# Chunked attention and a SoLU feed-forward layer on one core: the first two tiles take unsplit float32 weights

## The chip, the core and the metric

The kernel runs on one core of a Trainium2 chip. Its engines are TensorE (PE; its weight loads are listed as PEld), VectorE (DVE), ScalarE (ACT), GpSimd (POOL) and SyncE (SP, which here only issues transfers); 16 DMA engines move data. The metric is the device time of one execution in microseconds (us).

## The reference

For each of 8 x 8 heads, 576 rows are cut into nine chunks of 64; each chunk attends to itself only. The 4608 x 512 result goes through a feed-forward layer with SoLU and a layer norm.

```python
scores = scale * np.matmul(q_c, k_c.transpose(0, 1, 2, 4, 3))    # 64 x 64 per chunk
attn = softmax(scores);  out = np.matmul(attn, v_c)              # q, k, v: (8, 8, 576, 64) float32
x = np.ascontiguousarray(attn_out.transpose(0, 2, 1, 3)).reshape(B * S, H * D)   # 4608 x 512
h = x @ w_in                                                     # 512 x 1024
sm = e / (np.sum(e, axis=-1, keepdims=True) + 1e-09);  solu = h * sm
ln = (solu - mu) / np.sqrt(var + 1e-06) * g_ln
return (ln @ w_out).astype(np.float32)                           # 1024 x 512
```

w_in and w_out arrive as 64-bit floats and are turned into float32 on the chip; q, k, v and g_ln are 32-bit.

## The kernel before

**Tiles.** 36 tiles of 128 rows (two chunks each). For one tile: q and k are turned on TensorE (`nat` to `qT`, `kT`), the scores go to `sx` or `sy` in PSUM, VectorE and ScalarE make the softmax in `e`, TensorE turns it (`attn_t`), and a product with `v_sb` gives the tile of x, turned, again in `sx` or `sy`. The first product with w_in fills `ph` (two PSUM banks, one buffer); SoLU reads `ph` three times (VectorE's maximum `h_nmax`, ScalarE's exponential, VectorE's product into `z`), and only then may the next tile write `ph`. z is turned (`z_t` by transfers, or on TensorE for tiles 0, 1 and 35), and the second product, with w_out scaled by g, goes to `po`, in thirds of eight instructions. The store scales by `r` into `o_sb`.

**Split products.** TensorE's one-pass mode (fp32r) drops low bits, so each operand is held as two fp32r halves: x as `x_h`, `x_l`, w_in as `wi_h`, `wi_l`, w_out as `wo_h`, `wo_l`, z as `z_h`, `z_l`. A product is three passes: high by low, high by high, low by high. One tile takes 24 instructions of 128 x 512 for `ph` and 24 for `po`.

**Weights.** They come in eight parts called units: 0 to 3 are 128 rows of w_in, 4 to 7 are 256 rows of w_out, 1 MB each in `w_raw`. A unit is clipped (`unit_scale`, first half, on GpSimd), passed through Prelu (ScalarE), shifted and rounded to float32 in `w_a` (`unit_round`, VectorE), copied to its high part (`unit_high`, ScalarE), and the two low halves are the differences (`unit_rest`, VectorE).

**Order.** Each engine works strictly in the order in which the program issues. For tiles 0 to 4 and the weights this order is the string `START`: each word is a step, and a word that stands again continues the step where it yielded. `n` loads q and k of a tile, `v` its v, `P` a unit; `N` turns q or k, `S` scores, `A`, `B` the softmax (B's last part divides by the sum, "the norm"), `T` turns e, `V` the product with v and x's halves, `c`, `C`, `t`, `D` the four steps of a unit, `M` the first product, `X`, `Y` SoLU, `R` the variance, `z` and `Z` turn z, `F` a third of the second product, `o` the store, `U` prepares later tiles, `Q`, `q` load q and k of a later batch into `q_st`, `k_st`, `g` loads g_ln. "M:2" is M of tile 2, "D:3:1" the second low half of unit 3. From tile 5 on a loop issues all work: the first product of tile i, then three thirds for an earlier tile.

The tables `NV_DVE`, `MEAN_POOL`, `TV_DVE` and others say for single steps of the start whether VectorE, ScalarE or GpSimd takes them. `nat` has two buffers, so n:i waits until N:(i-2) is done; a unit's `w_raw` takes a place in the buffers of later tiles (`z_b`, `z_t`, `q_st`, `k_st`).

All instructions that the wrapper `Ordered` passes on carry one line in the profile, L49, that of the wrapper.

Of the kernel before, what the change touches and what calls it, by code (L numbers as in the profile page):

```python
# [57 lines left out]
def chunk_attention_then_solu_ffn(  # L58
# [103 lines left out]
    def unit_scale(x):  # L162

        hi = raws[x][:, :, :, 1]
        y = scaled[x] = work.tile([P, 2, HALF], F32, name="w_a", bufs=4)
        top = 1.875 * 2.0 ** 16  # L170
# [4 lines left out]
        act.activation(y, y, AF.Prelu, scale=2.0 ** -112, alpha=-(2.0 ** 32))

    def unit_round(x):
# [4 lines left out]
        kind, m = UNITS[x]  # L182
        if kind == "out" and m == 0:
            dve.tensor_scalar(
                out=g_sb, in0=g_sb, scalar1=1.0 / FF, scalar2=None, op0=ALU.mult
            )
# [505 lines left out]
    def product():  # L692
# [6 lines left out]
        "v": load_v, "g": load_g, "Q": load_batch, "q": load_some,  # L699
# [128 lines left out]
```

## Time and profile before

| what | us |
|---|---|
| median of 3 runs | 489.1 (488.9 to 489.53) |
| the profiled execution | 489.85 |
| its span, first to last instruction | 488.0 |
| TensorE busy | 466.7 (96%) |
| VectorE busy | 376.2 (77%) |
| ScalarE busy | 252.2 (52%) |
| GpSimd busy | 136.6 (28%) |

A row of the timeline has the start in us, the duration in us, the engine, the line, the operation, the tile written and the tiles read, the size, and how many instructions were merged; in brackets stands how long the engine idled before it and what ended that. "SPq" and "ACTq" are issues of transfers. Matmuls overlap, so the pace of TensorE is read from the distance of two starts.

### The profile page before, as it was taken

Reading aid. Unit: us, or ns where it says so; the run is one execution under the profiler, and the core shown is the slowest. Engines: PE = TensorE matmul, PEld = TensorE weight load, DVE = VectorE, ACT = ScalarE, POOL = GpSimd, SP = SyncE. Lnnn points to the kernel's source line nnn. Section 1 sums busy time; section 2 is a strip of 40 time slices with the busy share of each in tenths; the row PEclk is TensorE's granted clock in tenths of the full one; section 3 lists DMA queues with packets and bytes.
Section 4 is the critical chain, followed back from the end, with each engine's and each line's share of the span. In section 5 each row is a group of like instructions: output and inputs, shape, how many; then the busy total and the mean of one; then the engine's idle time right before and its main releaser. Section 6 shows DMA issues by size and latency. Waiting matters only on the chain.

```text
span 488.0 us, 11335 instructions
## 1 busy us (share of the span) xinstructions
PE 466.7 (96%) x4352; PEld 384.8 (79%) x4352; DVE 376.2 (77%) x525; ACT 252.2 (52%) x406; POOL 136.6 (28%) x287
## 2 busy tenths in 40 slices
PE   4599998999999999999999999999999999999996
PEld 3477886688888888888888888888888888888875
DVE  2989996797969797979797979797979797945420
ACT  3647872654546454546454545454545555554451
POOL 1302213332323232323232323232414141413300
PEclk9979999999999999999999999999999999999999
DMA  9999989569696887696538596949653534333211
GB/s 262 296 259 253 147 143 195 129 101 208 131 191 128 177 173 188 120 201 128 147 77 188 116 203 128 197 100 196 142 131 90 129 96 123 100 96 108 65 44 43
DMA packets 195909, 72.59 MB, mean 149 GB/s; under 512 B 180048, under 2 KB 180560, under 8 KB 195472
## 3 DMA queue, kind: packets, MB, share of 16 engines
q1 hardware_dynamic: 189008, 58.49, 55.2%
q0 software_dynamic: 6272, 12.60, 9.9%
q8 instruction: 34, 0.56, 0.5%
q10 hardware_dynamic: 576, 0.79, 0.5%
q14 instruction: 19, 0.16, 0.1%
HBM read 37.23 MB, written 9.44 MB: 96 GB/s over the span
## 4 chain that ended last, share of the span: by engine, by line
PE 82%; SPq 6%; DMA 4%; DVE 4%; ACT 2%; issue 1%; POOL 0%; ACTq 0%
PE po L49 39%; PE ph L49 36%; SPq L49 6%; PE sx L49 4%; DMA nat<-in_k_dram 3%; PE sy L49 3%; DMA k_st<-in_k_dram 1%; DVE h_nmax L49 1%; ACT z L49 1%; DVE e L49 1%; DVE z L49 1%; DVE w_a L49 0%; DVE s_sum L49 0%; ACT o_sb L49 0%; ACT wo_h L49 0%
## 5 line engine op out<-in xcount | busy, mean ns | idle before, releaser
L49 PE MATMUL ph<-wi_l,x_h 128*128 128x512 f32 x288 | 113.8, 395 | 0.3 <-DVE z L49 0.3
L49 PE MATMUL ph<-wi_h,x_h 128*128 128x512 f32 x288 | 113.0, 392 | 0.0
L49 PE MATMUL po<-wo_l,z_h 128*128 128x512 f32 x280 | 111.2, 397 | 0.1
L49 PE MATMUL po<-wo_h,z_l 128*128 128x512 f32 x280 | 109.5, 391 | 0.0
L49 PE MATMUL po<-wo_h,z_h 128*128 128x512 f32 x280 | 109.4, 391 | 0.0
L49 ACT ACTIVATE z<-ph,h_nmax 128x1024 f32<-128x1024 f32 x36 | 40.2, 1116 | 132.2 <-DVE h_nmax L49 132.1
L49 PE MATMUL ph<-wi_h,x_l 128*128 128x512 f32 x288 | 78.7, 392 | 0.0
L49 POOL DMA_DIRECT2D z_t<-z_b x136 | 67.6, 505 | 28.5 <-DVE z_b L49 24.5
L49 POOL TENSOR_TENSOR u<-ssq,eps 128x1 f32<-128x1 f32 x36 | 7.4, 205 | 230.4 <-ACT sq L49 230.3
L49 DVE TENSOR_REDUCE h_nmax<-ph 128x1 f32<-128x1024 f32 x36 | 44.0, 1223 | 34.6 <-PE ph L49 34.6
L49 PEld LDWEIGHTS ph<-wi_l,x_h 128*128 128x128 f32 x288 | 54.6, 190 | 12.0 <-ACT x_h L49 0.5
L49 PEld LDWEIGHTS ph<-wi_h,x_l 128*128 128x128 f32 x288 | 54.6, 190 | 11.5
L49 PEld LDWEIGHTS ph<-wi_h,x_h 128*128 128x128 f32 x288 | 54.7, 190 | 11.2
L49 PEld LDWEIGHTS po<-wo_l,z_h 128*128 128x128 f32 x280 | 52.5, 188 | 11.8 <-ACT z_h L49 0.5
L49 PEld LDWEIGHTS po<-wo_h,z_l 128*128 128x128 f32 x280 | 52.6, 188 | 11.4 <-DVE z_l L49 0.4
L49 PEld LDWEIGHTS po<-wo_h,z_h 128*128 128x128 f32 x280 | 52.6, 188 | 10.4
L49 DVE TENSOR_TENSOR z_l<-z_t,z_h 128x1024 fp32r<-128x1024 f32 (+1 forms) x35 | 40.7, 1163 | 21.6 <-ACT z_h L49 21.6
L49 ACT ACTIVATE z<-z,z_sum 128x1024 f32<-128x1024 f32 x35 | 40.4, 1153 | 29.6 <-DVE z L49 23.9
L49 DVE SCALAR_TENSOR_TENSOR z<-ph,z 128x1024 f32<-128x1024 f32 x36 | 43.9, 1220 | 12.8 <-ACT z L49 12.7
L49 DVE STREAM_TRANSPOSE z_b<-z 128x1024 f32<-128x1024 f32 x33 | 40.0, 1211 | 8.0 <-ACT z L49 7.8
L49 ACT ACTIVATE o_sb<-po,r 128x512 f32<-128x512 f32 (+1 forms) x37 | 24.7, 668 | 30.4 <-POOL r L49 20.2
L49 ACT ACTIVATE sq<-z 128x1024 bf16<-128x1024 f32 x36 | 37.5, 1043 | 0.0
(70 smaller groups left out, 591.0 us busy)
## 6 DMA issues: line engine op xcount, KB each, us to landing
out_dram<-o_sb SPq DMA_DIRECT2D x33, 256.0 KB, 2.5
v_sb<-in_v_dram SPq DMA_DIRECT2D x32, 256.0 KB, 4.4
z_t<-z_b SPq DMA_DIRECT2D x128, 64.0 KB, 2.9
z_t<-z_b POOLq DMA_DIRECT2D x128, 64.0 KB, 2.7
q_st<-in_q_dram SPq DMA_DIRECT2D x96, 72.0 KB, 3.3
k_st<-in_k_dram SPq DMA_DIRECT2D x96, 72.0 KB, 3.2
w_raw<-in_moe_w_out_dram SPq DMA_DIRECT2D x4, 1024.0 KB, 7.3
attn_t<-a_b SPq DMA_DIRECT2D x60, 64.0 KB, 3.9
```

The lines of the kernel that those rows point to most:

```text
L49: ins = make(*args, **kwargs)
```

## The change

- The first product of tiles 0 and 1 (`FM = 2`) reads the rounded float32 weights `w_a` directly, in float32, with an unsplit x (`x_f`): 8 instructions of 128 x 512 in place of 24. Tile 0's are issued in four parts, by 128 rows of w_in. The splitting of w_in comes behind them in the order; it is first used by tile 2. `w_a` has five buffers in place of four, and unit 3 takes the buffer of `z_b`.
- g_ln is loaded as eight rows on ScalarE's queue, turned on TensorE and scaled by 1/1024 from there; before, SP loaded it with one element per descriptor.
- The stores of tiles 0 and 1 go to SP as steps of their own; before, ScalarE issued them.
- GpSimd takes eleven of the low halves (`SUB_POOL`) and the norm of five tiles (`NORM_POOL`); VectorE takes two of the clippings (`CL_DVE`). `MEAN_POOL` and `TV_DVE` are emptied.
- Sixteen products of `ident` with itself into `ph` (`W`) stand among the first turns.
- `START` is a new order.

```diff
-    NV_DVE = ((1, 0), (6, 0), (8, 0), (9, 0), (9, 1),)
-    MEAN_POOL = (1,)
-    CL_DVE = ()
-    TV_DVE = (5,)
-    SUB_POOL = ()
-    NORM_POOL = ()
+    NV_DVE = ((0, 1), (1, 0), (1, 1), (7, 1), (9, 0),)
+    MEAN_POOL = ()
+    CL_DVE = (2, 6,)
+    TV_DVE = ()
+    SUB_POOL = ((0, 0), (1, 1), (2, 0), (2, 1), (3, 0), (3, 1), (4, 0), (4, 1), (5, 0), (7, 0), (7, 1),)
+    NORM_POOL = (1, 3, 4, 5, 7,)
+    XV_DVE = (1,)
+    FM = 2
...
+        tag, bufs = ("z_b", 1) if x == 3 else ("w_a", 5)
+        y = scaled[x] = work.tile([P, 2, HALF], F32, name="w_a", tag=tag, bufs=bufs)
...
     def start_values(i):
         values(i)
         yield
+        if i < FM:
+            x_whole(i)
+            return
...
+    def x_whole(i):
+        x = work.tile([P, NCC, P], F32, name="x_f", tag="x_h")
+        to = x.rearrange("p a (c t) -> p a c t", t=CH)
+        of = attn(i, 1).rearrange("p c a t -> p a c t")
+        if i in XV_DVE:
+            dve.tensor_copy(out=to, in_=of)
+        else:
+            act.copy(to, of)
+        st[i, "x"] = x, None
...
-        sums = [(n, cc, m) for n in range(2) for cc in range(NCC) for m in range(3)]
+        if i < FM:
+            ops = [(xh, None)]
+        else:
+            ops = [(xh, wi_l), (xh, wi_h), (xl, wi_h)]
...
             pe.matmul(
-                ph[:, n, :], x[:, cc, :], w[:, cc, cols],
+                ph[:, n, :], x[:, cc, :], scaled[cc][:, n] if w is None else w[:, cc, cols],
...
+    def warm(x):
+        if not idle:
+            idle.append(ps_h.tile([P, 2, HALF], F32, name="ph"))
+        for n in range(2):
+            pe.matmul(
+                idle[0][:, n, x % 4 * P:(x % 4 + 1) * P], ident, ident, start=True, stop=True
+            )
...
+    def start_store(i):
+        store(i)
+        yield
+        for to, of in stores:
+            sync.dma_start(to, of)
+        stores.clear()
...
-        sync.dma_start(g_sb, g_ln.rearrange("(a p) -> p a", p=P))
+        act.dma_start(g_row, g_ln.rearrange("(a p) -> a p", p=P))
+
+    def turn_g():
+        pt = bank()[:, :NFC]
+        pe.transpose(pt, g_row, ident[:NFC, :NFC])
+        yield
+        dve.tensor_scalar(out=g_sb, in0=pt, scalar1=1.0 / FF, scalar2=None, op0=ALU.mult)
```

What `START` and the tables make of each engine's order is shown at three places. The wrapper's line is L49 before and L50 now.

**TensorE, from the turns of tile 2 to the first products into `ph`** (`e_98`, `e_99`, `e_100` are the two softmax buffers; `ident` is the identity). Before:

```order
L49 MATMUL po<-ident,nat 128x128 x8
L49 MATMUL po<-ident,e_98 64x64 x16
L49 MATMUL sx<-kT,qT 64x64 x16
L49 MATMUL sy<-attn_t,v_sb 64x64 x16
L49 MATMUL po<-ident,nat 128x128 x8
L49 MATMUL ph<-wi_l,x_h 128x512
L49 MATMUL ph<-wi_h,x_h 128x512
```

Now:

```order
L50 MATMUL sy<-attn_t,v_sb 64x64 x16
L50 MATMUL po<-ident,e_100 64x64 x16
L50 MATMUL ph<-ident 128x128 x2
L50 MATMUL sx<-kT,qT 64x64 x16
L50 MATMUL ph<-w_a,x_f 128x512 x4
L50 MATMUL sy<-attn_t,v_sb 64x64 x16
L50 MATMUL po<-ident,nat 128x128 x4
L50 MATMUL po<-ident,e_99 64x64 x16
L50 MATMUL po<-ident,nat 128x128 x4
L50 MATMUL ph<-w_a,x_f 128x512 x4
```

Before, tile 0's first product stands behind the turns of tile 3 and reads split weights. Now its first half stands behind the scores of tile 3, and its second half behind the turns of tile 4, whose two groups stand between the halves.

**GpSimd, the steps of the start.** Before, the eight clippings and then only small steps:

```order
L355 MEMSET e_99 128x8
L49 TENSOR_SCALAR w_a<-w_raw 128x1024 x8
L49 TENSOR_SCALAR z<-z,z_sum 128x1024
L49 TENSOR_TENSOR u<-ssq,eps 128x1
L49 TENSOR_TENSOR r<-u,mhalf 128x1
```

Now, from the clippings of units 4 and 5 to that of unit 7:

```order
L50 TENSOR_SCALAR w_a<-w_raw 128x1024 x2
L50 TENSOR_TENSOR wi_l<-w_a,wi_h 128x512
L50 TENSOR_SCALAR w_a<-w_a,g_sb 128x512
L50 TENSOR_TENSOR wo_l<-w_a,wo_h 128x512
L50 TENSOR_TENSOR e_99<-e_99,s_rinv 128x8x64
L50 TENSOR_TENSOR wi_l<-w_a,wi_h 128x512 x3
L50 TENSOR_TENSOR e_100<-e_100,s_rinv 128x8x64
L50 TENSOR_SCALAR w_a<-w_a,g_sb 128x512
L50 TENSOR_TENSOR wo_l<-w_a,wo_h 128x512
L50 TENSOR_SCALAR w_a<-w_a,g_sb 128x512
L50 TENSOR_TENSOR wo_l<-w_a,wo_h 128x512
L50 TENSOR_SCALAR w_a<-w_raw 128x1024
```

The norms of tiles 4 and 5 (`e_99`, `e_100`) stand among subtractions, and the clipping of unit 7 behind all of these.

**SP, the later loads of the start.** Before:

```order
L49 DMA q_st<-in_q_dram 32x18x32 x8
L49 DMA k_st<-in_k_dram 32x18x32 x8
L49 DMA v_sb<-in_v_dram 128x8x64
L49 DMA nat<-in_q_dram 128x8x64
L49 DMA nat<-in_k_dram 128x8x64
L49 DMA k_st<-in_k_dram 32x18x32 x8
L49 DMA nat<-in_q_dram 128x8x64
L49 DMA nat<-in_k_dram 128x8x64
```

Now:

```order
L50 DMA nat<-in_q_dram 128x8x64
L50 DMA nat<-in_k_dram 128x8x64
L50 DMA q_st<-in_q_dram 32x18x32 x16
L50 DMA v_sb<-in_v_dram 128x8x64
L50 DMA nat<-in_q_dram 128x8x64
L50 DMA nat<-in_k_dram 128x8x64
L50 DMA k_st<-in_k_dram 32x18x32 x16
L50 DMA out_dram<-o_sb 128x512
L50 DMA z_t<-z_b 32x512 x8
```

Before, the q and k of tile 8 stand between the two halves of the k_st loads and those of tile 9 behind them; now tile 9 stands ahead of all q_st loads, tile 8 ahead of all k_st loads, and the store of tile 0 stands between these and the transfers of z.

More of the change, by code (lines that the diff above doesn't have):

```diff
@@ L121, in chunk_attention_then_solu_ffn @@
     g_sb = const.tile([P, NFC], F32, name="g_sb")
+    g_row = const.tile([NFC, P], F32, name="g_row")
     const.tile([P, 336], F32, name="pad")
@@ L168, in unit_scale @@
         hi = raws[x][:, :, :, 1]
-        y = scaled[x] = work.tile([P, 2, HALF], F32, name="w_a", bufs=4)
+        tag, bufs = ("z_b", 1) if x == 3 else ("w_a", 5)
+        y = scaled[x] = work.tile([P, 2, HALF], F32, name="w_a", tag=tag, bufs=bufs)
         top = 1.875 * 2.0 ** 16
@@ L177, in unit_round @@
     def unit_round(x):
[L182 to L186, printed above, removed]
         lo = raws.pop(x)[:, :, :, 0]
-        a = scaled.pop(x)
+        a = scaled[x]
         au = a.bitcast(U32)
-        dve.tensor_scalar(
+        (pool if x in SH_POOL else dve).tensor_scalar(
             out=au, in0=au, scalar1=3, scalar2=None, op0=ALU.logical_shift_left
@@ L197, in unit_round @@
         )
-        tops[x] = a
     def unit_high(x):
         kind, m = UNITS[x]
-        a = tops[x]
+        a = scaled[x]
         if kind == "in":
@@ L210, in unit_high @@
                 act.activation(top[:, y], a[:, y], AF.Copy, scale=g)
-        tops[x] = a, top
+        tops[x] = top
     def unit_rest(x, y):
         kind, m = UNITS[x]
-        a, top = tops[x]
+        a, top = scaled[x], tops[x]
         g = None
@@ L463, in ffn_in @@
         ph = st[i, "h"] = ps_h.tile([P, 2, HALF], F32, name="ph")
-        sums = [(n, cc, m) for n in range(2) for cc in range(NCC) for m in range(3)]
+        if i < FM:
+            ops = [(xh, None)]
+        else:
+            ops = [(xh, wi_l), (xh, wi_h), (xl, wi_h)]
+        last = len(ops) - 1
+        sums = [(n, cc, m) for n in range(2) for cc in range(NCC) for m in range(len(ops))]
         if i == 0:
@@ L471, in ffn_in @@
         for at, (n, cc, m) in enumerate(sums):
-            if i == 0 and at and at % 6 == 0:
+            if i == 0 and at and at % (2 * len(ops)) == 0:
                 yield
             cols = slice(n * HALF, (n + 1) * HALF)
-            x, w = ((xh, wi_l), (xh, wi_h), (xl, wi_h))[m]
+            x, w = ops[m]
             pe.matmul(
-                ph[:, n, :], x[:, cc, :], w[:, cc, cols],
-                start=(cc == 0 and m == 0), stop=(cc == NCC - 1 and m == 2),
+                ph[:, n, :], x[:, cc, :], scaled[cc][:, n] if w is None else w[:, cc, cols],
+                start=(cc == 0 and m == 0), stop=(cc == NCC - 1 and m == last),
+            )
+    idle = []
+    def warm(x):
[4 more added lines that the diff above has]
+                idle[0][:, n, x % 4 * P:(x % 4 + 1) * P], ident, ident, start=True, stop=True
             )
@@ L624, in store @@
             stores.append((out[i * P:(i + 1) * P, cols], o[:, cols]))
-        if not order.on or i >= NT - 3:
+        if order.on and i >= NT - 3:
             store_rest()
+    def start_store(i):
[4 more added lines that the diff above has]
+        stores.clear()
     stores = []
@@ L698, in chunk_attention_then_solu_ffn @@
         "P": load_pair, "P0": load_first, "P1": load_second, "n": load_natural,
[L699 removed]
+        "v": load_v, "g": load_g, "G": turn_g, "Q": load_batch, "q": load_some,
         "N": turn_natural, "S": scores, "A": start_softmax, "B": softmax_b,
@@ L702, in chunk_attention_then_solu_ffn @@
         "C": unit_round, "t": unit_high, "D": unit_rest, "M": ffn_in, "X": solu_a, "Y": solu_b,
-        "R": variance, "Z": z_turn, "z": z_half, "F": product, "o": store,
+        "R": variance, "Z": z_turn, "z": z_half, "F": product, "o": start_store, "W": warm,
     }
```

26 lines of the change are left out of this document (14 added, 12 removed).

## The prediction, made before the change was timed

> **What bounds the kernel now.** I read the page first (busy shares, then the slices), then the windows, and only then single rows.
>
> ```profile
> PE 466.7 (96%) x4352; PEld 384.8 (79%) x4352; DVE 376.2 (77%) x525; ACT 252.2 (52%) x406; POOL 136.6 (28%) x287
> PE   4599998999999999999999999999999999999996
> ```
>
> TensorE is busy 466.7 of 488.0 us, and the slices with a low digit are the first two or three and the last. The windows give what is missing there (columns: stretch, its length, busy time and count of PE, PEld, DVE, ACT, POOL, granted clock, DMA share, GB/s).
>
> ```profile
> 0.00:10.00 10.00, 3.72 (x43) 3.19 (x44) 0.69 (x1) 3.12 (x4) 1.96 (x11) 1.00 0.92 236
> 10.00:20.00 10.00, 6.56 (x81) 5.07 (x79) 9.74 (x13) 6.14 (x9) 2.44 (x2) 1.00 1.08 357
> 20.00:30.00 10.00, 6.63 (x82) 5.29 (x81) 9.92 (x15) 5.76 (x8) 1.54 (x1) 0.73 1.05 219
> 80.00:90.00 10.00, 7.05 (x66) 5.43 (x65) 9.65 (x16) 2.97 (x7) 4.16 (x8) 1.00 0.69 182
> 120.00:474.00 354.00, 353.92 (x3145) 292.78 (x3144) 277.89 (x386) 180.26 (x291) 106.49 (x230) 1.00 0.60 136
> ```
>
> From 120 to 474 us TensorE never rests, and the change leaves the program there as it is. So the change is worth what it does to the moment at which the loop's first product into `ph`, that of tile 5 (M:5), begins; everything behind it moves along. I follow TensorE to that moment.
>
> ```profile
> 26.07 1.09 PE L49 MATMUL po<-ident,nat 128*128 128x128 f32 x4 [0.82 <-DMA nat<-in_k_dram]
> 27.38 0.63 PE L49 MATMUL ph<-wi_h,x_h 128*128 128x512 f32 x1
> 27.81 0.63 PE L49 MATMUL ph<-wi_h,x_l 128*128 128x512 f32 x1
> ...
> 34.53 0.39 PE L49 MATMUL ph<-wi_h,x_h 128*128 128x512 f32 x1
> 34.76 0.40 PE L49 MATMUL ph<-wi_h,x_l 128*128 128x512 f32 x1
> ...
> 41.16 0.47 PE L49 MATMUL ph<-wi_l,x_h 128*128 128x512 f32 x1 [0.26 <-DVE z L49]
> ...
> 46.90 0.63 PE L49 MATMUL po<-ident,nat 128*128 128x128 f32 x4
> ...
> 51.00 0.50 PE L49 MATMUL ph<-wi_l,x_h 128*128 128x512 f32 x1
> ...
> 83.27 0.63 PE L49 MATMUL po<-ident,nat 128*128 128x128 f32 x4 [2.03 <-DMA nat<-in_q_dram]
> ...
> 86.67 0.66 PE L49 MATMUL po<-ident,nat 128*128 128x128 f32 x4 [0.91 <-DVE qT L49]
> ...
> 91.63 0.66 PE L49 MATMUL po<-ident,nat 128*128 128x128 f32 x4 [0.18 <-ACT kT L49]
> 92.04 0.48 PE L49 MATMUL ph<-wi_l,x_h 128*128 128x512 f32 x1
> ```
>
> Starts matter, not durations: 27.38 to 27.81 is 0.43 us for one 512-wide product, 34.53 to 34.76 is 0.23, so the clock was still half when M:0 began near 27. M:1 runs 41.16 to 46.90, M:2 begins at 51.00, M:5 at 92.04. Between M:2 and M:5 TensorE waits 2.03 + 0.91 + 0.18 = 3.1 us.
>
> **The change part by part.** *Loads.* What M:0 waits for is read where GpSimd takes up each unit of w_in (c:0 to c:3).
>
> ```profile
> 8.20 1.10 POOL L49 TENSOR_SCALAR w_a<-w_raw 128x1024 f32<-128x1024 f32 x1 [6.76 <-DMA w_raw<-in_moe_w_in_dram]
> 13.01 1.21 POOL L49 TENSOR_SCALAR w_a<-w_raw 128x1024 f32<-128x1024 f32 x1 [3.71 <-DMA w_raw<-in_moe_w_in_dram]
> 17.78 1.23 POOL L49 TENSOR_SCALAR w_a<-w_raw 128x1024 f32<-128x1024 f32 x1 [3.57 <-DMA w_raw<-in_moe_w_in_dram]
> 20.40 1.54 POOL L49 TENSOR_SCALAR w_a<-w_raw 128x1024 f32<-128x1024 f32 x1 [1.39 <-DMA w_raw<-in_moe_w_in_dram]
> 31.52 4.95 SPq L49 DMA_DIRECT2D g_sb<-in_moe_g_ln_dram  x1
> ```
>
> The last two lie 2.62 us apart with one unit between them; the steps before are 4.8 with a unit and a tile's q and k. So a unit costs 2.6, q and k of a tile 2.15, and v (half of that) 1.1, and the engines carry them one behind the other (DMA share 0.92 to 1.08). Tile 0 and unit 0 were there at 8.2. In the new queue order (n0 n1 w0 w1 n2 v0 n3 w3 w2 v1 n4 v2 n5) this makes: n1 7.7, w1 12.9, n2 15.0, n3 18.3, w3 20.9, w2 23.5, v1 24.6, n4 26.7, n5 30.0. The same rule puts the old n3 at 23.6 where the row says 26.07, because later loads share the engines: I keep up to 2.5 us for that in the range. g by rows moves off SP, where it held the queue for 4.95 us; the loads behind it then go out with no gap.
>
> *M:0.* Now it needs units that are scaled and rounded, not split. The last unit (w2) goes through these:
>
> ```profile
> 9.33 1.06 ACT L49 ACTIVATE w_a<-w_a 128x1024 f32<-128x1024 f32 x1 [1.30 <-POOL w_a L49]
> ...
> 15.60 0.64 DVE L49 TENSOR_SCALAR w_a<-w_a 128x1024 uint32<-128x1024 uint32 x1
> 16.76 1.30 DVE L49 SCALAR_TENSOR_TENSOR w_a<-w_raw,w_a 128x1024 uint16<-128x1024 uint32 x1
> 29.30 2.50 DVE L49 TENSOR_TENSOR wi_l<-w_a,wi_h 128x512 fp32r<-128x512 f32 x4
> ```
>
> Clipping on VectorE like the shift 0.65, Prelu 1.06, shift 0.64, rounding 1.3: 3.7 us, and about 1.6 of a softmax and a norm ahead in VectorE's queue: ready near 28.9, unit 3's rounding 1.3 later. The eight low-part halves at 0.62 (2.50/4) that stood before M:0 go behind it.
>
> One unsplit product is not in the trace. The program's other float32 products show two records for each (32 for 16), 64 columns wide:
>
> ```profile
> 57.31 0.66 PE L49 MATMUL po<-ident,nat 128*128 128x128 f32 x4
> 57.89 1.15 PE L49 MATMUL po<-ident,e 64*64 64x64 f32 x32
> 58.97 0.66 PE L49 MATMUL po<-ident,nat 128*128 128x128 f32 x4
> 59.56 0.69 PE L49 MATMUL sx<-kT,qT 64*64 64x64 f32 x32
> 60.07 0.65 PE L49 MATMUL sy<-attn_t,v_sb 64*64 64x64 f32 x32
> ```
>
> Sixteen turns of e take 58.97 - 57.89 = 1.08, 0.068 each; eight times the width gives 0.54 if they run one by one, 1.08 if its two quadrant pairs run side by side. Four passes of the 0.23 product lie between, at 0.91; I take that, since two records at a half-wide array point to the upper half. A tile is then 8 x 0.91 = 7.3 (4.3 to 8.6) against 24 x 0.23 = 5.5. So M:0's last two quarters run 28.9 to 32.5, where the old M:0 ended at 37.26 (below): 4.8 us earlier. Its first half (3.6 us near 23) has 2 us of slack before the 27 at which n4's turns follow. The 16 warm-up products fill waits for loads; at the slow pace they cost at most 16 x 0.43 = 6.9 us, about the 3.4 + 3.4 us that TensorE is idle in the second and third windows. If the clock is half anyway, M:0's tail takes 3.6 longer.
>
> *M:1 and the hold on `ph`.* `ph` has one buffer, so tile i+1 waits for three steps of tile i:
>
> ```profile
> 37.26 1.23 DVE L49 TENSOR_REDUCE h_nmax<-ph 128x1 f32<-128x1024 f32 x1 [1.65 <-PE ph L49]
> ...
> 38.52 1.12 ACT L49 ACTIVATE z<-ph,h_nmax 128x1024 f32<-128x1024 f32 x1 [0.18 <-DVE h_nmax L49]
> ...
> 39.79 1.22 DVE L49 SCALAR_TENSOR_TENSOR z<-ph,z 128x1024 f32<-128x1024 f32 x1
> ```
>
> From 37.26 to M:1 at 41.16 are 3.9 us. New: 32.5 + 3.9 + 7.3 = 43.7 for the end of M:1 (old 46.90). Then 24 turns (0.58 per four, from 58.97 to 59.56), one sx, one sy (0.51 each) and an e stand ahead of M:2: 24/4 x 0.5 + 1.0 + 1.1 = 5.0. M:2 at 48.7, 2.3 earlier.
>
> *M:2 to M:5.* Old 41.04. The 3.1 us of waits go: two of them come from the store of tile 0 on ScalarE's queue and the loads behind it:
>
> ```profile
> 78.57 0.37 ACTq L632 DMA_DIRECT2D out_dram<-o_sb  x1
> 78.99 1.15 ACT L49 ACTIVATE z<-z,z_sum 128x1024 f32<-128x1024 f32 x1 [5.21 <-DMA k_st<-in_k_dram]
> ```
>
> ScalarE stood 5.2 us behind that store's issue, which now stands on SP, where the next rows (halves of z_t) are wanted only behind M:5; tile 8's load now stands ahead of all k_st loads and tile 9's ahead of q_st. From the rows of the order, this stretch also loses two nat groups (1.2), an e (1.1), an sx and an sy (1.0) and gains a group of z turns (0.5): 2.8. So 35.2, and M:5 at 83.9: 8.1 earlier.
>
> *GpSimd's new work* is what must hide. It gets eleven subtractions, five of them with a scaling ahead, and five norms; VectorE loses 16 x 0.62 = 10 us net of small additions. A two-input step of 128x512 on GpSimd is not in the trace; the nearest row is its one-input step of twice the width:
>
> ```profile
> L49 POOL TENSOR_SCALAR w_a<-w_raw 128x1024 f32<-128x1024 f32 x8 | 9.9, 1234 | 40.4 <-DMA w_raw<-in_moe_w_in_dram 15.4 <-DMA w_raw<-in_moe_w_out_dram 14.2 <-ACT attn_t L49 6.7
> ```
>
> Half of 1.234 is 0.62 (T at least); twice that for two inputs is 1.24; twice again where VectorE gets in the way, 2.5. I take 1.24, the row read element for element over both inputs. The scaling counts T/2. Its longest chain starts when ScalarE has made wo_h of unit 4: ten ScalarE steps behind tile 0's exponential (34.8), half of them as wide as the row at 38.52 (1.1 us), half of half that width, 8.6 in all, and 0.8 of hand-overs: 44.2. From there 9.5 T pass until the first third of F:0 has its low parts, then c:7 (1.2), unit 7's Prelu, shift, rounding and scaled copy (4.2), and 3 T before the last third: with the 12.7 us of products from M:4 to M:5 and 1.2 for what lies between, M:5 can't be before 63.5 + 12.5 T. At 1.24 that is 79.0, hidden by 4.9 us; from T = 1.63 it sets the end, from 2.28 the change loses.
>
> **Sum.** -4.8 (M:0) + 1.6 (M:1's products) + 0.9 (what stands ahead of M:2) - 5.8 = -8.1 us. A new order has waits of its own; I charge 1.5, half of what the old one had. That leaves -6.6: 489.85 - 6.6 = 483.2 for a profiled execution, 482.5 for the median (489.1, 0.75 under the profiled execution).
>
> **Rivals.** *GpSimd becomes the bound* (slower). At T = 2.5 M:5 comes at 94.8, 2.7 late: 491.8; it decides from T = 2.28. For: the chain is long and in order, and norms that TensorE waits for stand behind subtractions. Against: 1.24 needs almost a doubling. 0.09. On this the Trainium skill speaks against the change: "GPSIMD Engine Reference", "Performance versus the Vector engine", has a two-input step take about twice VectorE's time, and "When to use GPSIMD" advises against it; an estimate from VectorE's 0.62 is T = 1.25 and the sum stays, while the port that the page has both engines share would lift it towards this rival, which no row here can show.
>
> *The front is won and partly given back* (gain 1 to 4, 485 to 488). Loads share the engines as the old n3 did (2.5), the clock stays half in M:0 (up to 3.6), or one of the tight places (the norm of tile 4 before M:2, unit 7's low parts) waits: 8.1 - 5 = 3 left, 486. For: DMA shares near 1 up to 80 us. 0.17.
>
> *Nothing moves* because 1.6 + 3.6 us of slow float32 products eat an M:0 that starts no earlier: 489. Against: four units' splitting, 5 us of VectorE, does leave the path. 0.06.
>
> **How the numbers follow.** Forecast 0.68: gain 4 to 10. The low end takes the cheaper float32 product (-3 on M:1) and no new waits, 478.5; the high end the second rival's 3 us less a little, 487.5. Repeats lie within 0.65 us of each other, so 0.2% (1.0 us) is the least that can be told from no change: faster 0.85, same 0.06, slower 0.09.
>
> **What would show it.** M:0's first unsplit product near 23 and its last end near 32.5; 0.91 us from one to the next; M:2 near 49 and M:5 near 84; no 5 us hole in ScalarE at the first store; POOL subtractions of 1.2 us. Wrong would be: M:5 later than 88, or subtractions over 2 us with `wi_l` or `wo_l` named as TensorE's releaser, or a new hole behind 120 us.

## The result: 3.0 us faster, not 6.6

The changed kernel takes 486.35 us (median of 4, 485.87 to 486.58) against 489.31 for the kernel before beside it on the same chip: a ratio of 0.9938, 95% interval 0.9920 to 0.9955, so 3.0 us are gained. The profiled execution takes 486.58 us, its span is 484.8 (before: 489.85 and 488.0).

From the page of the changed kernel, the busy shares and TensorE's slices:

```profile
PE 468.0 (97%) x4369; PEld 382.0 (79%) x4369; DVE 366.6 (76%) x509; ACT 253.1 (52%) x407; POOL 161.6 (33%) x305
PE   5889988999999999999999999999999999999996
```

VectorE lost 9.6 us and GpSimd gained 25. The windows of the changed kernel, with the columns of those shown of before:

```profile
20.00:30.00 10.00, 8.68 (x163) 5.87 (x155) 8.36 (x12) 5.92 (x9) 1.85 (x2) 1.00 1.08 276
...
120.00:474.00 354.00, 353.93 (x3089) 292.76 (x3082) 278.06 (x387) 180.92 (x292) 106.86 (x230) 1.00 0.59 134
```

From 20 to 30 us TensorE is busier and keeps its full clock (0.73 before); behind 120 us nothing changed (TensorE busy 353.92 before, 353.93 now), so the start of M:5 again tells the whole. TensorE of the changed kernel, from M:0 to M:5, with VectorE's first maximum of tile 0 between (timeline; start, duration, what was waited for):

```profile
23.94 3.70 PE L50 MATMUL ph<-w_a,x_f 128*128 128x512 f32 x8
...
29.66 0.63 PE L50 MATMUL po<-ident,nat 128*128 128x128 f32 x4 [0.82 <-DMA nat<-in_q_dram]
31.50 0.63 PE L50 MATMUL po<-ident,nat 128*128 128x128 f32 x4
31.96 3.60 PE L50 MATMUL ph<-w_a,x_f 128*128 128x512 f32 x8
35.40 0.60 PE L50 MATMUL po<-ident,nat 128*128 128x128 f32 x4
...
35.60 1.23 DVE L50 TENSOR_REDUCE h_nmax<-ph 128x1 f32<-128x1024 f32 x1 [2.07 <-PE ph L50]
...
39.39 7.13 PE L50 MATMUL ph<-w_a,x_f 128*128 128x512 f32 x16
46.36 1.04 PE L50 MATMUL po<-ident,nat 128*128 128x128 f32 x8
...
51.64 0.50 PE L50 MATMUL ph<-wi_l,x_h 128*128 128x512 f32 x1
...
62.05 0.50 PE L50 MATMUL po<-wo_l,z_h 128*128 128x512 f32 x1 [1.29 <-POOL wo_l L50]
...
74.95 0.50 PE L50 MATMUL po<-wo_l,z_h 128*128 128x512 f32 x1 [1.67 <-POOL wo_l L50]
...
88.83 0.48 PE L50 MATMUL ph<-wi_l,x_h 128*128 128x512 f32 x1
```

An unsplit product is again two records, so 16 records are eight products: 39.39 to 46.36 is 0.87 us each. M:5 begins at 88.83 instead of 92.04, 3.2 earlier, which is the difference of the spans. Set beside the prediction's steps (us; the end of M:0 is read as it was read for the kernel before, where VectorE begins `h_nmax`):

| step | before | forecast | measured |
|---|---|---|---|
| end of M:0 | 37.26 | 32.5 (-4.8) | 35.60 (-1.7) |
| from there to the end of M:1 | 9.64 | 11.2 (+1.6) | 10.76 (+1.1) |
| from there to M:2 | 4.10 | 5.0 (+0.9) | 5.28 (+1.2) |
| M:2 to M:5 | 41.04 | 35.2, and 1.5 charged (-4.3) | 37.19 (-3.8) |
| sum | | -6.6 | -3.2 |

The first row carries 3.1 of the 3.4 us that are missing. In the last, new waits took 2.96 us where 1.5 was charged, and the rest came out 1.0 better. Two readings of the changed kernel say why.

**The loads.** The first lines are GpSimd's and VectorE's clippings in the timeline, which wait for the units 1, 3 and 2; then the windows in between, whose last two columns are the DMA share and GB/s.

```profile
13.03 1.12 POOL L50 TENSOR_SCALAR w_a<-w_raw 128x1024 f32<-128x1024 f32 x1 [1.43 <-DMA w_raw<-in_moe_w_in_dram]
23.91 1.22 POOL L50 TENSOR_SCALAR w_a<-w_raw 128x1024 f32<-128x1024 f32 x1 [3.27 <-DMA w_raw<-in_moe_w_in_dram]
26.49 0.69 DVE L50 TENSOR_SCALAR w_a<-w_raw 128x1024 f32<-128x1024 f32 x1 [0.33 <-DMA w_raw<-in_moe_w_in_dram]
```

```profile
10.00:12.00 2.00, 1.64 (x11) 1.20 (x9) 1.97 (x4) 0.48 (x1) 1.13 (x1) 1.00 0.95 387
...
14.00:16.00 2.00, 0.91 (x9) 0.74 (x8) 1.97 (x4) 1.58 (x2) 0.15 (x1) 1.00 1.34 222
16.00:18.00 2.00, 2.00 (x41) 1.79 (x39) 1.97 (x4) 1.87 (x3) 0.00 (x0) 1.00 0.82 165
18.00:20.00 2.00, 1.15 (x38) 0.96 (x36) 0.51 (x1) 1.13 (x3) 1.91 (x2) 1.00 0.97 197
20.00:22.00 2.00, 2.00 (x65) 1.81 (x58) 1.74 (x3) 0.48 (x2) 0.63 (x1) 1.00 1.06 377
```

Unit 1 came as forecast (13.0 for 12.9); unit 3 came at 23.9 for 20.9 and unit 2 at 26.5 for 23.5. Where q, k and v run one behind the other (14 to 20 us) the engines move 165 to 222 GB/s, where units run 377 to 387.

**GpSimd.** Its groups of the first 90 us:

```profile
L50 POOL TENSOR_SCALAR w_a<-w_a,g_sb 128x512 f32<-128x512 f32 x5 | 9.2, 1846 | 7.7 <-ACT wo_h L50 7.7
L50 POOL TENSOR_TENSOR wi_l<-w_a,wi_h 128x512 fp32r<-128x512 f32 x6 | 8.1, 1356 | 0.5 <-ACT wi_h L50 0.5
...
L50 POOL TENSOR_TENSOR wo_l<-w_a,wo_h 128x512 fp32r<-128x512 f32 x5 | 6.4, 1276 | 0.4
L50 POOL TENSOR_TENSOR e<-e,s_rinv 128x512 f32<-128x512 f32 x5 | 5.7, 1147 | 11.4 <-DVE s_rinv L50 11.4
```

The subtractions take 1.28 to 1.36 us on the mean, near the assumed 1.24. The scaling by g ahead of a `wo_l`, with one input and a factor per partition, takes 1.85 on the mean (1.56 to 2.19): three times the assumed 0.62, and longer than the step with two inputs. The chain of waits runs through these steps from 45.96 to 74.95.

### The profile page after: what moved, and what is told of

Same layout as the page of the kernel before. It is cut to its first block, busy times and chain, and to the rows that moved or that the text cites. A ratio compares the mean times of both kernels' runs of the same rounds, so it can differ in the third digit from the quotient of the medians.

```text
span 484.8 us, 11379 instructions
## 1 busy us (share of the span) xinstructions
PE 468.0 (97%) x4369; PEld 382.0 (79%) x4369; DVE 366.6 (76%) x509; ACT 253.1 (52%) x407; POOL 161.6 (33%) x305
## 4 chain that ended last, share of the span: by engine, by line
PE 85%; POOL 4%; DMA 3%; DVE 2%; ACT 2%; SPq 1%; issue 1%; ACTq 0%; DVEq 0%; POOLq 0%
PE po L50 41%; PE ph L50 37%; PE sx L50 4%; PE sy L50 3%; DMA nat<-in_q_dram 2%; POOL w_a L50 2%; SPq L50 1%; POOL wo_l L50 1%; DMA nat<-in_k_dram 1%; POOL wi_l L50 1%; ACT wo_h L50 1%; DVE w_a L50 1%; ACT z L50 0%; POOL e L50 0%; ACT o_sb L50 0%
## 5 line engine op out<-in xcount | busy, mean ns | idle before, releaser
L50 PE MATMUL po<-wo_l,z_h 128*128 128x512 f32 x280 | 111.4, 398 | 3.0 <-POOL wo_l L50 3.0
L50 ACT ACTIVATE z<-ph,h_nmax 128x1024 f32<-128x1024 f32 x36 | 40.2, 1117 | 133.4 <-DVE h_nmax L50 133.4
L50 PE MATMUL po<-wo_h,z_l 128*128 128x512 f32 x280 | 109.6, 391 | 0.0
L50 PE MATMUL po<-wo_h,z_h 128*128 128x512 f32 x280 | 109.3, 390 | 0.0
L50 PE MATMUL ph<-wi_l,x_h 128*128 128x512 f32 x272 | 106.2, 391 | 0.0
L50 PE MATMUL ph<-wi_h,x_h 128*128 128x512 f32 x272 | 105.9, 389 | 0.0
L50 POOL TENSOR_TENSOR u<-ssq,eps 128x1 f32<-128x1 f32 x36 | 6.8, 190 | 217.2 <-ACT sq L50 217.2
L50 POOL DMA_DIRECT2D z_t<-z_b x136 | 67.9, 506 | 19.7 <-DVE z_b L50 16.8
L50 PE MATMUL ph<-wi_h,x_l 128*128 128x512 f32 x272 | 72.7, 389 | 0.0
L50 DVE TENSOR_REDUCE h_nmax<-ph 128x1 f32<-128x1024 f32 x36 | 44.1, 1224 | 37.6 <-PE ph L50 37.6
L50 PEld LDWEIGHTS po<-wo_l,z_h 128*128 128x128 f32 x280 | 52.5, 188 | 15.6 <-POOL wo_l L50 3.8
L50 PEld LDWEIGHTS po<-wo_h,z_l 128*128 128x128 f32 x280 | 52.6, 188 | 11.5 <-DVE z_l L50 0.4
L50 PEld LDWEIGHTS po<-wo_h,z_h 128*128 128x128 f32 x280 | 52.6, 188 | 10.3
L50 PEld LDWEIGHTS ph<-wi_h,x_l 128*128 128x128 f32 x272 | 51.1, 188 | 10.7
L50 PEld LDWEIGHTS ph<-wi_l,x_h 128*128 128x128 f32 x272 | 51.1, 188 | 10.6
L50 PEld LDWEIGHTS ph<-wi_h,x_h 128*128 128x128 f32 x272 | 51.1, 188 | 10.5
L50 DVE TENSOR_TENSOR z_l<-z_t,z_h 128x1024 fp32r<-128x1024 f32 (+1 forms) x35 | 40.7, 1163 | 22.5 <-ACT z_h L50 22.5
L50 DVE SCALAR_TENSOR_TENSOR z<-ph,z 128x1024 f32<-128x1024 f32 x36 | 44.0, 1221 | 14.9 <-ACT z L50 14.9
L50 ACT ACTIVATE z<-z,z_sum 128x1024 f32<-128x1024 f32 x36 | 41.5, 1153 | 22.6 <-DVE z L50 22.1
L50 DVE STREAM_TRANSPOSE z_b<-z 128x1024 f32<-128x1024 f32 x33 | 40.0, 1213 | 3.7 <-ACT z L50 3.4
L50 ACT ACTIVATE o_sb<-po,r 128x512 f32<-128x512 f32 (+1 forms) x37 | 24.7, 668 | 31.2 <-POOL r L50 20.3
L50 POOL DMA_DIRECT2D attn_t<-a_b x60 | 29.5, 499 | 25.0 <-PE ph L50 16.5
```

The costliest lines, as they stand in the source:

```text
L50: ins = make(*args, **kwargs)
```

## The experiments

A ratio is against the kernel before, run beside it on the same chip, whose medians were 488.97, 488.66, 489.07 and 488.99 us in the four batches; differences between kernels of different batches are taken from the ratios, at 489 us. The clock of a repeat is the mean granted clock of TensorE over that execution. The labels are those of the quoted expectations.

### GpSimd's share

**e1_out_low_dve**: the five halves of w_out go to VectorE.

```diff
-    SUB_POOL = ((0, 0), (1, 1), (2, 0), (2, 1), (3, 0), (3, 1), (4, 0), (4, 1), (5, 0), (7, 0), (7, 1),)
+    SUB_POOL = ((0, 0), (1, 1), (2, 0), (2, 1), (3, 0), (3, 1),)
```

> The changed kernel with the five low halves of w_out back on VectorE, where one step of about 0.7 us does what GpSimd does in a scaling (1.85 us) and a subtraction (1.28). Theory G (GpSimd's scaling steps hold back the thirds of tile 0's second product): TensorE's two waits on wo_l, 1.29 and 1.67 us, go; VectorE takes 3.5 us more between 44 and 75 us; M:5 moves from 88.8 to about 86, time about 483.5. Rival V (VectorE is full there, so the steps come late anyway or push the maximum and the product of SoLU): the waits change their name to VectorE and the time stays at 486 to 487.

Measured: 484.18 us, ratio 0.9901 (0.9888 to 0.9914), 1.8 us under the changed kernel. TensorE's waits between 38 and 120 us (total, times, longest):

```profile
PE ph L50 <- DVE z L50: 0.7, 1, 0.7
PE po L50 <- DVE z_l L50: 0.5, 1, 0.5
PE po L50 <- ACT qT L50: 0.2, 1, 0.2
```

The ratio's interval lies wholly below that of the changed kernel. Both waits on `wo_l` are gone, 1.4 us of smaller ones are left, and M:5 begins at 86.19. VectorE takes the five halves without a loss: in one instruction each, it does what GpSimd does in two (1.85 + 1.28).

**e2_scale_two_inputs**: GpSimd keeps its eleven halves, and the scaling is written as a step with two inputs.

```diff
-pool.tensor_scalar(out=of, in0=of, scalar1=g, scalar2=None, op0=ALU.mult)
+pool.tensor_tensor(out=of, in0=of, in1=g.to_broadcast([P, HALF]), op=ALU.mult)
```

> The changed kernel with GpSimd's five scalings by g written as a two-input product, g broadcast along the row, in place of a tensor_scalar with one scalar per partition. If it is the form that costs 1.85 us, the scaling falls to 1.05 to 1.3 us like the norms (two inputs, one broadcast), the chain up to F:0's first third is 1.8 us shorter, both waits on wo_l (1.29, 1.67) go or nearly, and the time is 483.5 to 484.5. If the 1.85 us come from VectorE working on the same memory at the time, the scaling stays above 1.6 and the time at 486.

Measured: 485.27 us, ratio 0.9919 (0.9899 to 0.9938). The scaling's group on GpSimd, and TensorE's wait on `wo_l`:

```profile
L50 POOL TENSOR_TENSOR w_a<-w_a,g_sb 128x512 f32<-128x512 f32 x5 | 6.7, 1332 | 7.6 <-ACT wo_h L50 7.6
```

```profile
PE po L50 <- POOL wo_l L50: 0.5, 1, 0.5
```

The same arithmetic on the same operands takes 1.33 us in place of 1.85, and the waits on `wo_l` fall from 3.0 to 0.5. Place by place the five scalings took 2.19, 2.04, 1.57, 1.88 and 1.56 us, and now take 1.68, 1.54, 1.04, 1.35 and 1.04: the form of the instruction costs 0.50 to 0.53 us at every place. Up to 0.64 more at some places is the same in both forms; what makes it was not tried. M:5 begins at 87.04, 1.8 earlier than in the changed kernel, but the time misses the expected 483.5 to 484.5, and by the ratios the gain of 0.9 us lies within the intervals.

**e3_no_gpsimd**: both tables emptied; VectorE takes all halves and norms.

```diff
-    SUB_POOL = ((0, 0), (1, 1), (2, 0), (2, 1), (3, 0), (3, 1), (4, 0), (4, 1), (5, 0), (7, 0), (7, 1),)
-    NORM_POOL = (1, 3, 4, 5, 7,)
+    SUB_POOL = ()
+    NORM_POOL = ()
```

> The changed kernel with all eleven low halves and the five norms on VectorE (both tables empty). The prediction's view (the offload frees 10 us of VectorE that the front needs): VectorE gets about 11 x 0.65 + 5 x 0.62 = 10 us more before 85 us, tiles 2 and 3 wait for low halves or for SoLU, the time goes to 488 to 491. Rival (the offload is not needed; VectorE has room and GpSimd only adds latency): no waits on GpSimd, 483 to 485.

Measured: 487.93 us, ratio 0.9987 (0.9977 to 0.9997). Now TensorE waits for VectorE instead (waits, 34 to 120 us):

```profile
PE po L50 <- DVE z_l L50: 2.0, 2, 1.8
PE po L50 <- DVE e L50: 1.3, 2, 1.1
PE ph L50 <- DVE z L50: 1.0, 2, 0.7
```

**e10_norms_dve**: on e1, the five norms go back to VectorE as well (`NORM_POOL = ()`).

> On the version without GpSimd's w_out halves (484.18 us): the five norms go back to VectorE as well, so that GpSimd keeps the six w_in halves alone. A norm is 1.15 us on GpSimd. Theory D (VectorE is the tight engine of the start, each norm costs it 0.6 to 0.7): five more steps, some 3 us more on VectorE before M:5, of which a third to a half reaches TensorE, as in the run with both tables empty (5 norms and 11 halves on VectorE: 487.93): 485.2 to 486. Rival (TensorE is late by GpSimd's slow norms as much as it would be by VectorE's fuller queue): 484.2 within 0.5.

Measured: 488.09 us, ratio 0.9984 (0.9958 to 1.0009), 4.1 us above e1, more than either theory expected. In its profiled execution TensorE waits 2.32 us for the qT of a later tile ahead of M:2; that qT stands on ScalarE behind an exponential of SoLU which had waited 2.12 us for VectorE's maximum. Behind the wait TensorE runs at half clock (windows; the number behind POOL's is the granted clock):

```profile
54.00:56.00 2.00, 2.00 (x34) 1.78 (x35) 2.00 (x4) 1.59 (x4) 1.13 (x1) 0.67 0.80 146
56.00:58.00 2.00, 2.00 (x6) 1.52 (x6) 1.92 (x4) 2.00 (x5) 0.00 (x0) 0.50 0.91 180
```

Only two of the ten repeats keep a clock of 0.999 or more (486.29 and 486.60); the other eight, at 0.992 to 0.996, take 487.36 to 490.91. So some 1.6 us of the 4.1 come with the fallen clock (an estimate: the median of all ten, 488.09, against that of the two, 486.45).

The runs give a ledger of GpSimd's new work, by their ratios: taking all of it is worth 2.4 us (0.9987 to 0.9938), taking only the six halves of w_in and the norms 4.2 (to 0.9901), the six halves without the norms nothing (0.9984). By this ledger VectorE is the tight engine at the norms, GpSimd at w_out; the part of the fallen clock is still in the value of the norms.

### The front

**e4_m0_ahead**: M:0's last quarters go ahead of tile 4's turns and tile 2's turns of e.

```diff
-A:3 P:4 B:2 V:1 c:2 N:4:0 C:3 c:2 P:5
-C:2 T:2 N:4:0 C:2 T:2 N:4:1 M:0 C:3 n:6 t:3 B:3 M:0 N:5:0
+A:3 P:4 B:2 V:1 c:2 C:3 c:2 P:5
+C:2 C:2 M:0 C:3 t:3 M:0 N:4:0 T:2 N:4:0 T:2 N:4:1 n:6 B:3 N:5:0
```

> The changed kernel with the last two quarters of M:0 ahead of the turns of tile 4's q and k and of T:2, on every engine. In the changed kernel these quarters start at 31.96, right behind the turn of k, which landed at 31.4; unit 2 is rounded at 30.3 and unit 3 at 31.5. Theory L (loads set M:0's end and all behind it moves along): M:0 ends 1.3 to 1.5 us earlier and M:5 about 1 earlier: 485.0 to 485.5. Theory G: M:0 ends earlier too, but TensorE's waits on wo_l grow by as much: 486 to 486.5.

Measured: 488.21 us (487.86 without one repeat of 944.86), ratio 0.9987 (0.9969 to 1.0005): 1.5 us (medians) to 2.4 (ratios) above the changed kernel, where either theory expected it no later than 486.5. TensorE in M:0's tail, and the windows around it:

```profile
31.46 5.40 PE L50 MATMUL ph<-w_a,x_f 128*128 128x512 f32 x8 [1.88 <-DVE w_a L50]
```

```profile
30.00:34.00 4.00, 2.54 (x4) 1.10 (x5) 3.93 (x7) 1.04 (x1) 0.42 (x1) 0.81 0.94 187
34.00:38.00 4.00, 4.00 (x35) 2.20 (x35) 1.67 (x2) 0.59 (x1) 2.09 (x2) 0.76 0.98 371
```

Without the turns ahead of it M:0's tail waits for rounded weights instead, and begins only 0.5 us earlier than in the changed kernel: VectorE takes up unit 2 at 27.56 in this execution, at 26.49 in the changed kernel, whose first rounding ended near 30.3 (an estimate: half of the two that run from 29.04 to 31.57). TensorE stands idle meanwhile and the clock falls, so that the tail takes 5.40 us in place of 3.60; the turns then follow behind it, and M:1 begins at 43.07 in place of 39.39.

**e5_one_load_less**: unit 2 isn't loaded; it reads unit 3's words, so its quarter of w_in is another, and 1 MB less is moved.

```diff
     def load_pair(x):
+        if x == 2:
+            raws[2] = raws[3]
+            return
```

> The changed kernel without the load of unit 2 of w_in: unit 3's words are used for unit 2 as well, so that part of the output is not the reference's, and 1 MB (2.6 us of load time) less stands ahead of tile 4's q and k. Theory L (the loads, three us later than forecast, set the end of M:0 and all behind it): M:0's last quarters start near 29.5 in place of 31.96, M:5 is 2 to 2.5 us earlier than 88.8, time 484.0 to 484.5. Rival (another chain, GpSimd's, sets M:5, and M:0's end has slack): TensorE's waits on wo_l grow, time 486 to 486.5.

Measured: 485.18 us, ratio 0.9919 (0.9889 to 0.9950). TensorE's M:0 tail and the two waits:

```profile
30.56 3.60 PE L50 MATMUL ph<-w_a,x_f 128*128 128x512 f32 x8
...
60.24 0.50 PE L50 MATMUL po<-wo_l,z_h 128*128 128x512 f32 x1 [1.13 <-POOL wo_l L50]
73.12 0.50 PE L50 MATMUL po<-wo_l,z_h 128*128 128x512 f32 x1 [1.64 <-POOL wo_l L50]
...
88.53 0.48 PE L50 MATMUL ph<-wi_l,x_h 128*128 128x512 f32 x1
```

The tail comes 1.4 us earlier, and up to the second wait the rest follows by 1.4 to 1.8; GpSimd's waits stay nearly as they are, because its chain moves along. Behind the second wait the granted clock falls to 0.50 (76 to 78 us), and M:5 begins at 88.53, only 0.3 earlier. Two of the four repeats keep a clock of 0.999 or more and take 484.03 and 484.36 us, as the first theory has it; the other two, at 0.996, take 486.0 and 486.49. So the loads do hold M:0's tail in the changed kernel: here TensorE waits for none of them between its two halves. By how much is rough: the tails of e7 and e2, whose start is that of the changed kernel, begin at 31.22 and 32.23. Nor could the tail come much earlier: M:0's first half begins at 24.14, and from there to 30.56 TensorE does not rest.

**e9_unit3_earlier**: on e1, unit 3's load goes ahead of v of tile 0 and of q and k of tile 3.

```diff
-... A:0 v:0 n:3 W:4 c:0 c:1 W:9 W:10 B:0 c:0 P:3 N:2:1 ...
+... A:0 P:3 v:0 n:3 W:4 c:0 c:1 W:9 W:10 B:0 c:0 N:2:1 ...
```

> On the version without GpSimd's w_out halves (484.18 us): the load of unit 3 moves ahead of v of tile 0 and of q and k of tile 3, so that n2, v0 and n3 no longer run in a row; nothing else moves. Theory R (loads of short packets behind one another run at about 215 GB/s and a unit between them fills the engines): w2 is there 1 to 1.5 us earlier, M:0's tail at 30.3 to 30.8 instead of 31.57, M:5 a microsecond earlier: 483.0 to 483.5. Rival 1 (bytes alone count; w2 has the same bytes ahead of it): 484.2, tail at 31.5. Rival 2 (q and k of tile 3, which TensorE wants at 18.9, come 2.6 later; everything up to M:0's first half in TensorE's order moves along, and its tail too): tail at 32 to 33.5, 485 to 486.

Measured: 486.83 us, ratio 0.9951 (0.9931 to 0.9972). TensorE waits for the q of tile 3 in its place:

```profile
21.76 0.72 PE L50 MATMUL po<-ident,nat 128*128 128x128 f32 x4 [4.06 <-DMA nat<-in_q_dram]
...
34.68 3.60 PE L50 MATMUL ph<-w_a,x_f 128*128 128x512 f32 x8
```

The second rival came true in its mechanism: 2.4 us lost, the tail 3.1 later than in e1, both a little more than it expected. Whether mixing large and small loads would raise the rate stays open, since VectorE took up unit 2 only behind tile 3's late softmax.

**e6_no_warm** and **e11_e1_no_warm**: the sixteen warm-up products are left out, of the changed kernel and of e1.

```diff
     for word in START.split():
+        if word[0] == "W":
+            continue
```

> The changed kernel without the sixteen warm-up products of ident. If they hold the clock up for M:0: its first half (four unsplit products, 3.6 us from 23.9) runs at half pace, ends near 31 in place of 27.6, the turns of tile 4 follow near 31.5 in place of 29.66, M:0's end and M:5 are 1 to 2 us later: 487.3 to 488.3. If the loads hide it all (tile 4's q lands at 29.6 anyway): within 0.5 us of 486.35.

> On the version without GpSimd's w_out halves (484.18 us), which has no TensorE wait over 0.7 us behind M:0: the sixteen warm-up products are left out. Theory W0 (they only fill waits for loads; M:0's first half is hidden behind loads at either clock): 484.2 within 0.5, M:0's tail at 31.3 to 31.7. Rival W1 (without them the clock is half until M:0's tail, 3.6 us longer): 486 to 488. Without waits over 1 us no granted clock under 0.9 is expected between 40 and 120 us, and repeats within 1 us of each other.

Measured: 486.92 us, ratio 0.9962 (0.9944 to 0.9981), for e6, its repeats scattered (485.09 to 488.61) around the changed kernel's 486.35; 483.74 us, ratio 0.9904 (0.9881 to 0.9927), for e11, the same as e1 within its interval. So the warm-ups neither gain nor cost what could be measured here: without them M:0's first half begins at 24.33 in e11, its tail at 30.75 and M:5 at 85.99 (e1: 86.19). With e1 this is the fastest version found, 1.7 us below the changed kernel.

The scatter of e6 goes with the granted clock: the five repeats at 0.999 or 1.000 lie between 485.09 and 486.72, the five at 0.993 to 0.996 between 487.12 and 488.61. The profiled execution, one of the second five, shows where the clock falls. TensorE behind the second wait on `wo_l`:

```profile
74.29 0.50 PE L50 MATMUL po<-wo_l,z_h 128*128 128x512 f32 x1 [1.60 <-POOL wo_l L50]
...
76.17 0.63 PE L50 MATMUL ph<-wi_h,x_h 128*128 128x512 f32 x1
76.60 0.63 PE L50 MATMUL ph<-wi_l,x_h 128*128 128x512 f32 x1
```

From one product to the next are 0.43 us, for about 3 us: the half clock, which the changed kernel's profiled execution does not show behind its wait of 1.67. The warm-ups do not prevent it: e7 (below) has them and the same waits, and five of its ten repeats stand at 0.995 or 0.996. In e1 and e11, whose waits in this stretch are below 1 us, no repeat is below 0.998. A wait of 1.6 us thus costs its length and, in some executions, 1.7 to 2.4 us more (the distance of the two groups' medians in e7 and e6); what decides between them, the runs do not show.

**e8_g_by_element**: g goes back to SP, one element per descriptor, behind the loads of tile 5.

> The changed kernel with g loaded on SP by single elements, as in the kernel before, behind tile 5's q and k. The prediction's term: SP's queue is held for up to 4.95 us there, units 4 and 5 and all behind them land 3 to 5 us later, GpSimd's chain starts as much later: M:5 2 to 4 us later, 488 to 490. Rival (the loads behind it have that much slack, since GpSimd's chain waits on ScalarE): 486 to 486.8.

Measured: 487.36 us, ratio 0.9974 (0.9954 to 0.9994), 1.0 us (medians) to 1.8 (ratios) above the changed kernel, between what the two theories expected. SP's issue of it:

```profile
29.67 1.21 SPq L50 DMA_DIRECT2D g_sb<-in_moe_g_ln_dram  x1
```

It takes 1.21 us, not the 4.95 of before, so most of those were not the load's own price; that they were a queue full with what stood ahead is only argued. Moving g was worth no more than the 1.0 to 1.8 us.

### The late part: stores and loads

**b1_before_late_part**: the kernel before, with two edits of the change alone: the stores of tiles 0 and 1 on SP, and the last eight k_st loads behind q and k of tile 9. **b2** has only the loads, **b3** only the stores.

```diff
-T:5 X:3 Y:3 o:0 V:4 q:8 T:5 n:9 Y:3 Z:3 z:1:1 M:4 z:1:1
+T:5 X:3 Y:3 o:0 V:4 T:5 n:9 q:8 Y:3 Z:3 z:1:1 M:4 o:0 z:1:1
...
-        "R": variance, "Z": z_turn, "z": z_half, "F": product, "o": store,
+        "R": variance, "Z": z_turn, "z": z_half, "F": product, "o": start_store,
```

> The kernel before with only the late part of the change: the stores of tiles 0 and 1 issued on SP as steps of their own, and the last eight k_st loads behind the q and k of tile 9. The prediction counts 3.1 us of TensorE's waits between M:2 and M:5 for that, all gone: M:5 at 89 in place of 92.04, 486 to 486.5. Rival (the waits go to another place, since SP then holds the store and VectorE is full there): 488 to 489.

Measured: 486.36 us, ratio 0.9948 (0.9931 to 0.9965). The waits on tile 9's q, on qT and on kT are gone, and M:5 begins 3.65 earlier than before (92.04) in the profiled executions, the 3.1 us of the prediction and a little more:

```profile
88.39 0.48 PE L49 MATMUL ph<-wi_l,x_h 128*128 128x512 f32 x1
```

By the ratio the gain is 2.5 us, within the intervals what the whole change gains. Which of the two edits does it?

> Kernel before with the order of the late loads alone: the last eight k_st loads stand behind q and k of tile 9, everything else (the stores on ScalarE too) as before. Theory L (the order of the loads makes the 3.1 us of waits, as the run with the stores back on ScalarE suggests, where no hole was left): no ScalarE hole over 2 us behind the first store, M:5 at 88.4 to 89.5 instead of 92.04, 486 to 487. Rival S (the store on ScalarE's queue makes the hole of 5.2 us, and 0.91 + 0.18 of the waits with it; the loads only the 2.03 us on tile 9's q): hole still 4 to 6 us, M:5 at 90 to 91, 487.5 to 488.5.

Measured: 490.40 us, ratio 1.0037 (1.0023 to 1.0052): slower. ScalarE of b2:

```profile
73.88 0.69 ACT L49 ACTIVATE o_sb<-po,r 128x512 f32<-128x512 f32 x1 [0.21 <-PE po L49]
80.47 0.40 ACTq L632 DMA_DIRECT2D out_dram<-o_sb  x1
80.92 1.15 ACT L49 ACTIVATE z<-z,z_sum 128x1024 f32<-128x1024 f32 x1 [6.35 <-DMA k_st<-in_k_dram]
```

The store holds ScalarE until a k_st load has landed. With that load 2 us later the hole grows from 5.21 to 6.35, and the wait moves to `z_l`, 2.93 us on TensorE.

> Kernel before with the stores of tiles 0 and 1 on SP, behind the transfers of z, and nothing else: the loads stay in the old order. Theory L (the order of the loads makes the waits): the 2.0 us wait of TensorE on tile 9's q stays, M:5 at 91 to 92, 488 to 489. Rival S (the store on ScalarE's queue makes the hole): hole gone, waits of 0.91 and 0.18 gone, and since ScalarE's z no longer comes late the 2.03 may be all that is left: M:5 at 90 to 91, 487.5 to 488.

Measured: 487.11 us (486.53 to 491.97), ratio 0.9965 (0.9951 to 0.9979). ScalarE's hole is gone, and the transfer is waited for instead; TensorE of b3:

```profile
85.38 1.08 PE L49 MATMUL po<-ident,nat 128*128 128x128 f32 x4 [4.23 <-DMA nat<-in_q_dram]
```

The profiled execution is the longest of the seven (491.97), with half the clock behind that wait; the others lie between 486.53 and 488.21. The stores alone gain 1.7 us, the loads alone lose 1.8, both together gain 2.5. So the loads lose while the store waits for them; whether they gain anything once it does not, 0.8 us by these ratios, lies within the intervals of b1 and b3.

**e7_stores_act**: the changed kernel with the stores of tiles 0 and 1 issued by ScalarE again.

```diff
-        if order.on and i >= NT - 3:
+        if not order.on or i >= NT - 3:
             store_rest()
```

> The changed kernel with one part undone: ScalarE issues the stores of tiles 0 and 1 again, in its own queue, where kernel before had a 5.21 us hole behind the first of them; the loads stay in the new order. Theory L3 (the prediction's term: the waits behind that store are 3.1 us, and the store alone makes them): 486.4 + 3 = 489.4 us, with a hole of 4 to 5 us on ScalarE behind the first store and two or three TensorE waits between M:2 and M:5 beside those on wo_l. Rival (the order of the loads makes them: ScalarE's issue is held only while k_st and q_st loads fill the engines, and q and k of tiles 8 and 9 now stand ahead of those): hole under 2 us, 486.4 to 487.

Measured: 486.70 us, ratio 0.9961 (0.9939 to 0.9982): by the intervals not to be told from the changed kernel. ScalarE of e7:

```profile
75.19 0.69 ACT L50 ACTIVATE o_sb<-po,r 128x512 f32<-128x512 f32 x1 [1.58 <-PE po L50]
75.91 0.38 ACTq L669 DMA_DIRECT2D out_dram<-o_sb  x1
76.34 1.15 ACT L50 ACTIVATE z<-z,z_sum 128x1024 f32<-128x1024 f32 x1 [0.46 <-DVE e L50]
```

No hole, though SP issues k_st loads until 78.60 in this run. So the store does not wait for whatever load is under way. That it waits for a certain one, which in this order had landed by then, would fit, but is not shown. Why a store of `o_sb` waits for a load of `k_st` at all, no row of these traces says; that stays open.

## Why the prediction was wrong

The sign, the range (478.5 to 487.5) and the stage were right; the gain was forecast more than twice too large. By its steps:

- **"M:0's last two quarters run 28.9 to 32.5": failed, by 3.1 us.** The two quarters take 3.4 us (3.6 forecast), but begin at 31.96. Two terms were wrong. The load model priced each load by itself and had the queue go out with no gap: from unit 1 to unit 3 it had 8.0 us (12.9 to 20.9), and 10.9 passed (13.03 to 23.91); tile 4's q, forecast for 26.7, was waited for until 29.66. Between its two halves TensorE waited 0.50 us for a v and 0.82 for that q; without these waits, in e5, the tail begins 1.4 us earlier. The other 1.7 stand in TensorE's own queue: the prediction dated the tail by the rounded weights alone and took the first half to have 2 us of slack, but even in e5 that half begins at 24.14 and not near 23, and it, a product with v and three groups of turns fill TensorE without a gap until 30.56. The split is rough, since tails of one and the same start scatter by 1 us. Why the loads are slow in this stretch was only argued from the windows. The prediction had seen the same of the old tile 3 (26.07 for 23.6) and kept 2.5 us for it in the range, not in the sum: it belonged in the sum.
- **"One unsplit product ... 0.91": right**, 0.87. M:1 ends 10.76 us behind M:0 (11.2 forecast), and what stands ahead of M:2 takes 5.28 (5.0; its own terms add up to 5.1). So M:2 comes 0.64 us later than before, not 2.3 earlier: M:1's slow products and the longer work ahead of M:2, +2.3 together, are more than the 1.7 that M:0 won.
- **"The scaling counts T/2": failed.** It measured 1.85 us, not 0.62, on the mean of five, and the chain began at 45.96 instead of 44.2. To F:0's first third it took 16.1 us (45.96 to 62.05) in place of 9.5 T = 11.8, and 3.9 of that difference are its three scalings. Where the bound was 79.0 and hidden, `wo_l` came late twice, 2.96 us; 1.5 was charged for new waits. e2 shows that the form of the step makes 0.5 us of each scaling; even its two-input form took 1.33 on the mean, twice what was counted. T itself, 1.24, was right (1.28), so the first rival failed by the rule that it named and came half true by a term that nobody priced. The Trainium skill, "GPSIMD Engine Reference", "Performance versus the Vector engine", has a two-input step take about twice VectorE's time, and 1.28 against 0.62 to 0.70 us agrees. Its "When to use GPSIMD" calls one-input steps roughly line-rate; the 1.85 us of this scaling does not agree.
- **"The 3.1 us of waits go": right**, and so was the pair of causes (the store on ScalarE and the loads behind it): b1 gains 2.5 us with nothing else. By b3 the stores make 1.7 of it; the loads alone lose (b2), and their 0.8 beside the stores is not clear of the noise. What it took for a property of ScalarE's queue is one of the order, though: e7 has the store there without a hole.
- **"The 16 warm-up products fill waits": right** as far as can be measured (e6, e11).
- The likeliest case should have been the rival "the front is won and partly given back" (486), which had 0.17: loads, a tight place, 3 us left. It named all but the scaling and TensorE's own work ahead of M:0's tail.

The sum, then: in kernel before, the late part alone brings as much as the whole change, within the intervals (ratios 0.9948 and 0.9938). By that the new front, with GpSimd's work in it, costs about what it saves; with GpSimd's w_out halves on VectorE the whole gains 1.7 to 1.8 us more (e1, e11). The parts do not simply add up: the stores on SP, worth 1.7 us in kernel before, are worth nothing measurable in the changed one (e7).

## What to carry to other kernels

Price a load by the stretch of loads it stands in, not by its size; date a step by its engine's own queue as well as by its inputs; and put a lateness that the trace of before shows already into the sum rather than into the range. Price every form of an instruction on the engine that is to run it: here a one-input scaling took three times what was assumed, and longer than a two-input step of the same size, and a chain of such steps multiplies it. And take edits apart in the old kernel too: here one edit alone lost 1.8 us, the other won 1.7, the pair won 2.5.
